# Two MoE layers behind attention, one core: conversions tied in place, stores and first loads divided

## The chip, the cores and the metric

One core of a Trainium2 chip runs the kernel. The metric is the device time of one execution in microseconds. Three executions of the kernel before took 878.22 us in the median (874.89 to 879.35).

## What is computed

Attention of four batches, eight heads and 32 global and 512 local tokens: each local token sees the global ones and a window of 32 to either side, each global token sees all. Its output, 2176 rows of 512, goes through two feed-forward layers (512 to 2048 to 512), all in float32. The weights arrive as float64 words, which the kernel turns into float32 itself.

```python
x = out_attention.transpose(0, 2, 1, 3).reshape(B * S, H * D)
h = x @ moe_w_in
x = (np.maximum(h, 0) + alpha * np.minimum(h, 0)) @ moe_w_out
h = x @ moe2_w_in
out = (h * np.clip(h + 3, 0, 6) / 6) @ moe2_w_out
```

## The kernel before

Products are made of values split into a high and a low part (`wt[:, m, 0]`, `wt[:, m, 1]`), three matmuls for each product. The 2176 tokens go through layer 1 in five blocks of 512, 512, 512, 256 and 384 columns (`blocks`, L331). The main loop (L779) runs, for each block, 16 chunks of the hidden size: `h_tile` (L365), `act` (L371 to L385) and, LAG = 2 steps later, `y_tiles` (L396). Block 0 has two lanes of 256 columns, the second DELAY = 4 steps behind the first (steps 4 to 15 run both), since its tokens' attention ends later. At step 4 the loop finishes that attention and transposes its output (L796 to L798).

Attention (`local_units`) works on 32 units of loads q, k and v, scores, exponentials, transposes, a copy of these to SBUF (L209) and values; `attention_steps` advances it between the chunks. All first loads are issued by SyncE's queue (SP), in the order of L231 to L239.

**Conversions.** A half chunk of weights is loaded as int64 words into one of four buffers `raw` (L97). `to_float32` then takes ScalarE L108 and VectorE L111, L112 and L114; L120 and L121 (layer 1) or L460 and L463 (layer 2) split the result `z` (two buffers). Layer 1's 32 halves are converted in block 0 by `Weights.convert`: of the two that belong to a step one is written ahead of `h_tile` and one behind `act`, two steps before they are used. Layer 2's conversions are a generator, `second_weights`, of 159 steps: 6 to begin with, then 13 for each of eight in-parts, then three (convert, high part, low part) for each of 16 `out_parts`, and a last one for the last store; each conversion stores its result to DRAM. `SPLIT` gives the steps of each block, spread evenly over the block's loop. A buffer `raw` is free again when L114 has read it (layer 1) or when its store has landed (layer 2). In block 4 `inputs` also reads the stored results of blocks 0 to 2 back into `xq` and splits them (L562, L563).

**Order.** Each engine runs its instructions in one order, and so does SP's queue of DMAs. That order is a planner's: it lists what is written, estimates times of its own, and issues next what it believes to be ready, earliest written first. `tc.keep_in_program_order(ins)` adds one edge: `ins` comes behind the instruction that was written just before it on its engine. In the kernel before, `second_weights` hands it to `to_float32` as `here`; `split_w` (layer 1) doesn't, so there L108 and L111 are free to go ahead.

**Stores.** At the end of a block, two L833 stores write four column groups of `x2` to DRAM. At the end of layer 2, `to_rows` copies each PSUM bank to SBUF (`evacuate`: ScalarE for even places, VectorE for odd ones) and stores it; the last three are the global rows "g" (four batches of 32 rows, L644), (3, 1, 0) and (3, 1, 1) (L648).

Of the kernel before, what the change touches and what calls it, by code (L numbers as in the profile page):

```python
# [10 lines left out]
F32R = mybir.dt.float32r  # L11
# [6 lines left out]
B, H, SL, SG, D = 4, 8, 512, 32, 64  # L18
# [6 lines left out]
W = 32  # L25
# [9 lines left out]
FIRST_UNITS = HP  # L35
# [4 lines left out]
DELAY = 4  # L40
STEPS = [[2] * 4 + [1] * 16, [1] * 16, [1] * 16, [2] * 16, [0] * 16]
CONVERT = (5, 7, 9)
SPLIT = (0, 46, 46, 30, 37)
STREAM = 4


# [6 lines left out]
def fused_kernel(ctx, tc, qT, kE, vE, qgT, kN, vN, vgN, w1, alpha, w2, mask, ident, out):  # L53
    nc = tc.nc
# [14 lines left out]
    spare = {"y": True, "n": 0}  # L69

    def load_constants():
        nc.sync.dma_start(out=mask_sb, in_=mask)
        nc.sync.dma_start(out=ident_sb, in_=ident)
        nc.sync.dma_start(out=alpha_sb, in_=alpha)
        nc.vector.tensor_scalar(out=c1_sb, in0=alpha_sb, scalar1=-1.0, scalar2=1.0, op0=ALU.mult, op1=ALU.add)

# [20 lines left out]
        nc.sync.dma_start(out=raw, in_=src[j, :, 512 * m:512 * m + 512])  # L97
        return raw

    def to_float32(raw, here=lambda ins: ins):  # L100

        words = raw.bitcast(U32).rearrange("p (f two) -> p f two", two=2)
        low, high = words[:, :, 0], words[:, :, 1]
        here(nc.scalar.activation(low, low, AF.Relu, bias=quarter_sb, scale=0.9 * 2.0 ** -29))  # L108
        z = work.tile([128, 512], F32, tag="z", name="z", bufs=ZB)
        bits = z.bitcast(U32)  # L110
        here(nc.vector.tensor_scalar(out=z, in0=high.bitcast(F32), scalar1=2.0 ** -112, scalar2=None, op0=ALU.mult))  # L111
        nc.vector.scalar_tensor_tensor(out=bits, in0=bits, scalar=3, in1=low, op0=ALU.logical_shift_left,  # L112
                                       op1=ALU.bitwise_or)
        nc.vector.scalar_tensor_tensor(out=bits, in0=high, scalar=0x80000000, in1=bits, op0=ALU.bitwise_and,  # L114
                                       op1=ALU.bitwise_or)
        return z
# [41 lines left out]
    def local_units(att):  # L158
        units = [(b, hf, hp) for b in range(B) for hf in range(2) for hp in range(HP)]
        q_t, k_t, v_t, p_t, rs_t, pt_t = {}, {}, {}, {}, {}, {}  # L160
        def load(u):
            b, hf, hp = units[u]
            q_t[u] = att.tile([128, 256], F32, tag="q", name="q_t", bufs=PRE + 1)
            nc.sync.dma_start(out=q_t[u], in_=qT[b, hp, :, 256 * hf:256 * hf + 256])
            k_t[u] = att.tile([128, UNIT_K], F32, tag="kE", name="k_t", bufs=PRE + 1)
            nc.sync.dma_start(out=k_t[u], in_=kE[b, hp, :, 384 * hf:384 * hf + UNIT_K])

# [280 lines left out]

    def second_weights():

        here = tc.keep_in_program_order
        todo = [(j, 0) for j in range(NJ)] + [(j, 1) for j in range(NJ)]
        raws, pending = [], []

# [21 lines left out]

        fetch()  # L480
        yield
        fetch()
# [1 line left out]
            yield  # L484
        for m in range(NP):
            own = raws.pop(0)
            z0, own = to_float32(own, here), own.bitcast(F32R)
            yield
            high(z0, own)
            yield  # L490
            low(z0, own, in_parts[m][:, 0])
            yield
            own = raws.pop(0)
            z1, own = to_float32(own, here), own.bitcast(F32R)
            store()
            yield
            high(z1, own)
            yield
            low(z1, own, in_parts[m][:, 1])
            yield  # L500
            a, b, c, d = z0[:, 0:256], z0[:, 256:512], z1[:, 0:256], z1[:, 256:512]
            add(d, c, d)
            add(c, a, c, ALU.subtract)
            store()
            yield
            st = parts_tile()
            high(z1, st)
            yield
            low(z1, st, in_parts[m][:, 2])
            fetch()  # L510
            yield
            add(a, d, a, ALU.subtract)
            add(b, b, a, ALU.subtract)
            store()
            yield
            st = parts_tile()
            high(z0, st)
            yield
            low(z0, st, in_parts[m][:, 3])
            fetch()  # L520
            yield
            store()
            yield
        for j in range(NJ):
            own = raws.pop(0)
            z, own = to_float32(own, here), own.bitcast(F32R)
            store()
            yield
            high(z, own)
            fetch()  # L530
            yield
            low(z, own, out_parts[j])
            yield
# [105 lines left out]
    def to_rows(y, tiles, order=None):  # L639
        for c in order or range(len(tiles)):  # L640
            tile_ = tiles[c]
            r = evacuate(y[c], c, 512, ("t", "z"))
            if tile_ == "g":
                nc.sync.dma_start(out=rows[:, 0:SG, :], in_=r)  # L644
            else:
                bb, hf, i = tile_
                at = SG + 256 * hf + 128 * i
                nc.sync.dma_start(out=rows[bb, at:at + 128, :], in_=r)  # L648
# [130 lines left out]
    for bi in range(len(blocks)):  # L779
# [49 lines left out]
        for c in range(0, NC, 2):  # L829
            r = work.tile([128, 2, 512], F32, tag="g", name="ev", bufs=LAG + 1)[:, :, :n]  # L830
            nc.scalar.copy(r[:, 0, :], y[c][:, :n])
            nc.vector.tensor_copy(r[:, 1, :], y[c + 1][:, :n])
            nc.sync.dma_start(out=x2[bi][:, c:c + 2, :], in_=r)  # L833
        xt = xt_next

    second_layer(bt)
# [56 lines left out]
```

## Time and profile before

| | us |
|---|---|
| median of three executions | 878.22 |
| lowest, highest | 874.89, 879.35 |
| the profiled execution | 876.12 |
| its span, first to last instruction | 874.3 |
| TensorE matmul busy | 843.5 (96%) |
| VectorE busy | 527.2 (60%) |
| ScalarE busy | 388.9 (44%) |

Engines: PE is TensorE's matmuls, PEld its weight loads, DVE is VectorE, ACT is ScalarE, SP is SyncE, SPq its queue of DMA issues. L108 is line 108 of the kernel. A row of waits gives who waited for whom. A DMA share of 1 would be all of the core's 16 DMA engines busy.

### The profile page before, as it was taken

How to read it: one execution, taken by the hardware profiler on the slowest of the kernel's cores; microseconds unless marked ns; L12 is line 12 of the kernel's file. 1: busy time of each engine (PE TensorE's matmuls, PEld its weight loads, DVE VectorE, ACT ScalarE, POOL GpSimd, SP SyncE). 2: the span in 40 equal slices, each digit the busy share in tenths (PEclk: the TensorE clock that was granted, in tenths of full speed). 3: DMA queues.
4: the chain of work that ended last, by engine and by line, in shares of the span. 5: the costliest groups of instructions: out<-in, count | busy, mean ns of one | idle time of the engine just before them, and what ended most of it. 6: DMA issues, size and time to landing. Idle time of an engine off the chain costs nothing.

```text
span 874.3 us, 17112 instructions
## 1 busy us (share of the span) xinstructions
PE 843.5 (96%) x6728; PEld 731.1 (84%) x6728; DVE 527.2 (60%) x1267; ACT 388.9 (44%) x893; POOL 0.2 (0%) x4
## 2 busy tenths in 40 slices
PE   7889989999999999999999999999999999999996
PEld 5679989877887878788999977888888999988995
DVE  5989885565567556576687975766720766701321
ACT  6767564454445444354555543433410444401221
POOL 0000000000000000000000000000000000000000
PEclk8889999999999999999999999999999999999998
DMA  9986662335547451688766577666786888788781
GB/s 315 322 277 211 203 221 86 132 98 197 180 150 264 163 169 74 233 306 280 266 227 213 183 250 266 220 208 219 239 300 219 275 269 299 266 307 296 251 255 41
DMA packets 63875, 195.63 MB, mean 224 GB/s; under 512 B 7220, under 2 KB 19764, under 8 KB 62772
## 3 DMA queue, kind: packets, MB, share of 16 engines
q1 hardware_dynamic: 63796, 194.55, 66.5%
q8 instruction: 53, 0.87, 0.4%
q14 instruction: 26, 0.21, 0.1%
HBM read 160.44 MB, written 34.08 MB: 222 GB/s over the span
## 4 chain that ended last, share of the span: by engine, by line
PE 75%; DMA 11%; DVE 8%; ACT 4%; issue 1%; SPq 1%; ACTq 0%; DVEq 0%
PE o_ps L636 21%; PE h_ps L365 15%; PE y_ps L396 14%; PE k_ps L690 14%; DMA raw<-in_w 5%; PE h_ps L755 4%; DMA wo<-raw 3%; PE s_ps L184 2%; DVE z L112 1%; PE o_ps L219 1%; PE pt_ps L207 1%; DVE z L114 1%; DVE t L377 1%; ACT raw L108 1%; DMA ws<-wi 1%
## 5 line engine op out<-in xcount | busy, mean ns | idle before, releaser
L396 PE MATMUL y_ps<-g,wt 128*128 128x256 f32 (+2 forms) x1152 | 212.4, 334 | 7.2 <-ACT g L383 7.2
L365 PE MATMUL h_ps<-xt,wt 128*128 128x256 f32 (+2 forms) x1152 | 209.9, 333 | 3.7 <-DVE t L377 3.0
L365 PEld LDWEIGHTS h_ps<-xt,wt 128*128 128x128 f32 x1152 | 181.3, 194 | 20.6 <-ACT wt L120 3.2
L396 PEld LDWEIGHTS y_ps<-g,wt 128*128 128x128 f32 x1152 | 175.3, 190 | 26.8 <-ACT g L383 8.9
L690 PE MATMUL k_ps<-bt,ws 128*128 128x512 f32 (+1 forms) x672 | 140.6, 363 | 0.0
L690 PEld LDWEIGHTS k_ps<-bt,ws 128*128 128x128 f32 x672 | 121.9, 188 | 15.0 <-issue 0.4
L636 PE MATMUL o_ps<-ws,g 128*128 128x512 f32 x480 | 117.8, 391 | 1.6 <-DMA ws<-wo 1.6
L636 PEld LDWEIGHTS o_ps<-ws,g 128*128 128x128 f32 x480 | 89.6, 188 | 19.3 <-DMA ws<-wo 2.1
L377 DVE SCALAR_TENSOR_TENSOR t<-t,c_sb,h_ps 128x256 f32<-128x256 f32 (+2 forms) x96 | 55.4, 589 | 76.9 <-ACT t L375 76.9
L375 ACT ACTIVATE t<-h_ps 128x512 f32<-128x512 f32 (+2 forms) x84 | 43.1, 515 | 83.2 <-PE h_ps L365 83.1
L636 PE MATMUL o_ps<-ws,far 128*128 128x512 f32 x336 | 76.8, 389 | 0.0
L636 PEld LDWEIGHTS o_ps<-ws,far 128*128 128x128 f32 x336 | 63.1, 188 | 13.1
L383 ACT CAST g<-t 128x512 fp32r<-128x512 f32 (+2 forms) x84 | 45.2, 538 | 41.9 <-DVE t L377 39.9
L108 ACT ACTIVATE raw<-raw,quarter_sb 128x512 uint32<-128x512 uint32 x64 | 49.0, 768 | 28.4 <-DMA raw<-in_w 28.4
L384 DVE TENSOR_TENSOR g<-t,g 128x512 fp32r<-128x512 f32 (+2 forms) x84 | 49.2, 586 | 19.2 <-ACT g L383 19.1
L628 ACT ACTIVATE t<-cd,half_sb 128x512 f32<-128x512 f32 (+1 forms) x32 | 21.5, 671 | 72.6 <-DVE cd L675 71.6
L196 ACT ACTIVATE p<-p,st 128x128 f32<-128x128 f32 x128 | 49.9, 391 | 7.1 <-DVE st L192 7.0
L112 DVE SCALAR_TENSOR_TENSOR z<-z,raw 128x512 uint32<-128x512 uint32 x64 | 44.0, 688 | 2.2 <-ACT raw L108 0.9
L405 DVE COPY ev<-o_ps 128x512 f32<-128x512 f32 x7 | 4.8, 690 | 66.7 <-PE o_ps L636 66.7
L114 DVE SCALAR_TENSOR_TENSOR z<-raw,z 128x512 uint32<-128x512 uint32 x64 | 43.9, 686 | 0.6
L630 ACT CAST g<-t 128x384 fp32r<-128x384 f32 (+1 forms) x48 | 26.3, 549 | 26.4 <-DVE t L629 26.4
L631 DVE TENSOR_TENSOR g<-t,g 128x384 fp32r<-128x384 f32 (+1 forms) x48 | 28.8, 600 | 12.4 <-ACT g L630 11.3
(97 smaller groups left out, 822.8 us busy)
## 6 DMA issues: line engine op xcount, KB each, us to landing
ws<-wi SPq DMA_DIRECT2D x80, 512.0 KB, 5.0
ws<-wo SPq DMA_DIRECT2D x80, 512.0 KB, 4.6
raw<-in_w SPq DMA_DIRECT2D x64, 512.0 KB, 4.7
v_t<-in_vE SPq DMA_DIRECT2D x32, 512.0 KB, 5.1
wi<-raw SPq DMA_DIRECT2D x16, 512.0 KB, 3.0
wi<-parts SPq DMA_DIRECT2D x16, 512.0 KB, 4.1
wo<-raw SPq DMA_DIRECT2D x16, 512.0 KB, 5.0
k_t<-in_kE SPq DMA_DIRECT2D x32, 240.0 KB, 4.1
```

The source lines that it names most:

```text
L108: here(nc.scalar.activation(low, low, AF.Relu, bias=quarter_sb, scale=0.9 * 2.0 ** -29))
L112: nc.vector.scalar_tensor_tensor(out=bits, in0=bits, scalar=3, in1=low, op0=ALU.logical_shift_left, op1=ALU.bitwise_or)
L114: nc.vector.scalar_tensor_tensor(out=bits, in0=high, scalar=0x80000000, in1=bits, op0=ALU.bitwise_and, op1=ALU.bitwise_or)
L196: nc.scalar.activation(p[:, n, :], p[:, n, :], AF.Exp, bias=st[:, 1, n:n + 1], scale=-1.0, accum_out=st[:, 2, n:n + 1])
L365: nc.tensor.matmul(ps[:, a:b], lhsT=wts[j][:, 0, wl, 128 * c:128 * c + 128], rhs=xt[c][:, xl, a:b], start=k == 0, stop=k == 3 * NC - 1)
L375: nc.scalar.activation(t[:, a:b], ps[:, a:b], AF.Relu, scale=-1.0)
L377: nc.vector.scalar_tensor_tensor(out=t[:, c:d], in0=t[:, c:d], scalar=c1_sb[:, j:j + 1], in1=ps[:, c:d], op0=ALU.mult, op1=ALU.add)
L383: nc.scalar.copy(g[:, 0, a:b], t[:, a:b])
L384: nc.vector.tensor_tensor(out=g[:, 1, a:b], in0=t[:, a:b], in1=g[:, 0, a:b].bitcast(F32), op=ALU.subtract)
L396: nc.tensor.matmul(y[c][:, a:b], lhsT=wts[j][:, 1, wl, 128 * c:128 * c + 128], rhs=g[:, gl, a:b], start=first, stop=last)
L636: nc.tensor.matmul(y[c], lhsT=g[:, gl, 128 * c:128 * c + 128], rhs=wo[:, wl, :], start=j == 0 and (wl, gl) == (0, 0), stop=j == NJ - 1 and ...
L690: nc.tensor.matmul(bank, lhsT=wt[:, wl, at:at + 128], rhs=bt[x][:, c, xl, 0:w], start=k == 0, stop=k == 5)
```

## The change

`here` becomes the tie for every call of `to_float32`, layer 1's too. `SPLIT` moves twelve steps of `second_weights` from block 4 to blocks 1 and 2. `mask`, `ident` and the q loads of the first four units are issued by ScalarE's queue in place of SP's. The store of the global rows becomes four stores of 32 rows, on SP and ScalarE in turn, and each store of two `x2` column groups becomes two.

```diff
-SPLIT = (0, 46, 46, 30, 37)
+SPLIT = (0, 52, 52, 30, 25)
...
     def load_constants():
-        nc.sync.dma_start(out=mask_sb, in_=mask)
-        nc.sync.dma_start(out=ident_sb, in_=ident)
+        nc.scalar.dma_start(out=mask_sb, in_=mask)
+        nc.scalar.dma_start(out=ident_sb, in_=ident)
         nc.sync.dma_start(out=alpha_sb, in_=alpha)
...
-    def to_float32(raw, here=lambda ins: ins):
+    here = tc.keep_in_program_order
+
+    def to_float32(raw):
...
         def load(u):
             b, hf, hp = units[u]
             q_t[u] = att.tile([128, 256], F32, tag="q", name="q_t", bufs=PRE + 1)
-            nc.sync.dma_start(out=q_t[u], in_=qT[b, hp, :, 256 * hf:256 * hf + 256])
+            early = nc.scalar if u < FIRST_UNITS else nc.sync
+            early.dma_start(out=q_t[u], in_=qT[b, hp, :, 256 * hf:256 * hf + 256])
...
-            z0, own = to_float32(own, here), own.bitcast(F32R)
+            z0, own = to_float32(own), own.bitcast(F32R)
...
             if tile_ == "g":
-                nc.sync.dma_start(out=rows[:, 0:SG, :], in_=r)
+                for b in range(B):
+                    queue = nc.scalar if b % 2 else nc.sync
+                    queue.dma_start(out=rows[b, 0:SG, :], in_=r[W * b:W * b + W, :])
...
-            nc.sync.dma_start(out=x2[bi][:, c:c + 2, :], in_=r)
+            for i in range(2):
+                nc.sync.dma_start(out=x2[bi][:, c + i, :], in_=r[:, i, :])
```

## Rows read from the trace of the kernel before

**Rows 1.** The page, busy tenths in 40 slices of the span: TensorE.

```profile
PE   7889989999999999999999999999999999999996
```

**Rows 2.** Stages: from:to length, busy PE PEld DVE ACT POOL, clock, DMA share, GB/s.

```profile
24.00:57.00 33.00, 29.39 (x443) 23.55 (x443) 30.59 (x106) 24.12 (x72) 0.00 (x0) 0.91 0.89 305
57.00:136.00 79.00, 73.89 (x854) 70.95 (x854) 68.44 (x176) 51.25 (x121) 0.00 (x0) 0.96 0.63 205
136.00:160.00 24.00, 24.00 (x363) 22.79 (x362) 10.28 (x46) 10.95 (x38) 0.00 (x0) 1.00 0.34 109
160.00:372.00 212.00, 212.00 (x1891) 170.43 (x1889) 124.41 (x332) 100.10 (x249) 0.00 (x0) 1.00 0.50 168
430.00:530.00 100.00, 94.06 (x516) 88.67 (x515) 82.59 (x151) 51.89 (x99) 0.00 (x0) 0.98 0.71 237
```

**Rows 3.** Waits, 0:136 us, then 430:530: total, times, longest.

```profile
ACT raw L108 <- DMA raw<-in_w: 22.7, 19, 2.8
...
ACT bt L562 <- DMA xq<-x: 8.5, 2, 4.7
ACT raw L108 <- DMA raw<-in_w: 5.7, 2, 5.0
```

**Rows 4.** Timeline, TensorE: start, length, work, [idle before <- what ended it].

```profile
7.77 0.64 PE L184 MATMUL s_ps<-k_t,q_t 64*32 64x128 f32 x16 [2.04 <-DMA k_t<-in_kE]
34.23 1.21 PE L396 MATMUL y_ps<-g,wt 128*128 128x256 f32 x8 [1.04 <-ACT g L383]
58.35 1.54 PE L350 MATMUL xt_ps<-ident_sb,xo 128*128 128x128 f32 x6 [3.05 <-ACT pt L209]
...
126.85 1.43 PE L365 MATMUL h_ps<-xt,wt 128*128 128x256 f32 x10 [3.00 <-DVE t L377]
```

**Rows 5.** Timeline, ScalarE, in front of three of these.

```profile
31.86 0.76 ACT L108 ACTIVATE raw<-raw,quarter_sb 128x512 uint32<-128x512 uint32 x1 [0.77 <-DMA raw<-in_w]
...
57.08 0.74 ACT L108 ACTIVATE raw<-raw,quarter_sb 128x512 uint32<-128x512 uint32 x1 [2.77 <-DMA raw<-in_w]
...
124.57 0.74 ACT L108 ACTIVATE raw<-raw,quarter_sb 128x512 uint32<-128x512 uint32 x1 [2.21 <-DMA raw<-in_w]
```

**Rows 6.** Groups: count | busy, mean ns; L120: min/median/max ns, first, last start.

```profile
L112 DVE SCALAR_TENSOR_TENSOR z<-z,raw 128x512 uint32<-128x512 uint32 x64 | 44.0, 688 | 2.2 <-ACT raw L108 0.9
...
L111 DVE TENSOR_SCALAR z<-raw 128x512 f32<-128x512 f32 x64 | 26.8, 419 | 0.0
...
L120 ACT CAST wt<-z x32: 600/608/633, 16.1 to 134.3; 128x512 fp32r<-128x512 f32 x32
```

**Rows 7.** Timeline, TensorE, block 4.

```profile
482.52 3.06 PE L396 MATMUL y_ps<-g,wt 128*128 128x384 f32 x12 [1.91 <-ACT g L383]
...
508.68 2.37 PE L396 MATMUL y_ps<-g,wt 128*128 128x384 f32 x12 [1.88 <-ACT g L383]
...
527.98 2.34 PE L636 MATMUL o_ps<-ws,g 128*128 128x512 f32 x9 [1.64 <-DMA ws<-wo]
```

**Rows 8.** Timeline, first loads, ScalarE's first exponential; a window as in rows 2.

```profile
1.64 0.43 SPq L72 DMA_DIRECT2D mask_sb<-in_mask  x1
...
3.53 0.43 SPq L166 DMA_DIRECT2D k_t<-in_kE  x1
...
6.34 0.40 ACT L196 ACTIVATE p<-p,st 128x128 f32<-128x128 f32 x1 [4.34 <-DVE st L192]
...
4.00:6.00 2.00, 1.73 (x34) 0.65 (x32) 0.13 (x1) 0.00 (x0) 0.00 (x0) 1.00 0.88 202
```

**Rows 9.** Tail: last issues; windows as in rows 2; L648's landing near 674.

```profile
867.38 0.94 SPq L648 DMA_DIRECT2D out<-ev  x2
...
870.00:871.00 1.00, 0.00 (x0) 0.00 (x0) 0.00 (x0) 0.00 (x0) 0.00 (x0) 0.50 0.88 301
871.00:872.00 1.00, 0.00 (x0) 0.00 (x0) 0.00 (x0) 0.00 (x0) 0.00 (x0) 0.50 0.29 104
...
DMA to landing us min/median/max: 2.9/3.0/3.0
```

More of the change, by code (lines that the diff above doesn't have):

```diff
@@ L449, in second_weights @@
     def second_weights():
-        here = tc.keep_in_program_order
         todo = [(j, 0) for j in range(NJ)] + [(j, 1) for j in range(NJ)]
@@ L493, in second_weights @@
             own = raws.pop(0)
-            z1, own = to_float32(own, here), own.bitcast(F32R)
+            z1, own = to_float32(own), own.bitcast(F32R)
             store()
@@ L525, in second_weights @@
             own = raws.pop(0)
-            z, own = to_float32(own, here), own.bitcast(F32R)
+            z, own = to_float32(own), own.bitcast(F32R)
             store()
```

## The prediction

> **What bounds the kernel now.** I read the page's slices first: TensorE is at 9 tenths in almost every slice [rows 1]. So time can only be won where TensorE stands still or runs on the lower clock. The table by stage says where that is [rows 2]: 160 to 372 us is full, as is what lies behind 530 us [rows 1]; 24 to 57 us lose 3.6 us, 57 to 136 us lose 5.1 us and have a mean clock of 0.96, 430 to 530 us lose 5.9 us and have 0.98. Before 24 us and behind the last matmul lie the start and the tail.
>
> The waits of the two poor stages name the suspect [rows 3]: up to 136 us ScalarE waited 22.7 us in 19 pieces for raw weights (L108, the first step of a conversion), more than for anything else there; from 430 to 530 us it waited 5.7 us for raw weights and 8.5 us for the blocks that `inputs` reads back (L562). TensorE's own idle rows show when that hurts [rows 4]: 1.04 us before 34.23, 3.05 us before 58.35, 3.00 us before 126.85. Each has, on ScalarE just ahead, an L108 that waited for a raw landing: 0.77, 2.77 and 2.21 us [rows 5]. Counting L108 and L209 in the order of the code, the L108 at 57.08 is the fourteenth, written behind step 5's activation, and the copy L209 that it held up is written in step 4. At 57 us four L108 had run ahead of their place. That is the planner at work: L108 and L111 depend on a load alone, so it puts them wherever it believes the load has landed.
>
> **The change part by part.** Sums go against the profiled execution: 876.12 us, of which 874.3 is the span; it lies 2.1 us under the median of the three (878.22), so the same sum is taken from the median.
>
> *Ties of layer 1's conversions.* No instruction is added. L108 and L111 of the 32 conversions may no longer run ahead of the instruction written before them on ScalarE and VectorE. Where a free L108 waits for its load, the activations, attention copies and exponentials of its step stand queued behind it, and TensorE waits for those; a tied one stands behind them, and what waits for it is h two steps on. The raw load that takes over its buffer is issued later too, and on SP's queue q, k and v of units two ahead stand behind that load: 0 (+1). Early: the 1.04 us before 34.23 goes, since the L108 in front (0.77 of waiting and 0.76 of work, [rows 5]) is then written behind step 1's activation: -1.0 us (0 to -1.0). The 3.05 us before 58.35: the conversion is written a step behind the copy, so the copy isn't held: -3.0 us (0 to -3.05). The rest of 57 to 136 us: 3.7 us of TensorE idle behind 58.35 and 0.04 x 79 = 3.2 us of clock, 6.9 us to be had. VectorE sets a floor there. A conversion costs it 0.42 + 3 x 0.69 = 2.48 us (L111, L112 and two more like L112) [rows 6]. It was busy for 68.4 of the 79 us [rows 2]. Two conversions that ran ahead (`z` has two buffers, so their VectorE part can't run further ahead) now fall into this stage: 68.4 + 5.0 = 73.4 us. Unless work slips behind 136 us, where VectorE was busy for only 10.3 of 24 us [rows 2], the stage can't be shorter than that: at most -5.6 us, of which 1.4 are already counted before 58.35, so -4.2 to 0. I take two thirds, -2.8: it reached 93% at most over such a stretch (30.6 of 33 us, [rows 2]), so the floor itself won't be met without that slip. New waits from the new order of everything: the nearest rows are the present idle times of 1 to 3 us [rows 4]; one of the size in between, +2.0 us (0 to +6).
>
> *Split of layer 2's conversion.* Twelve of the 159 steps leave block 4 (37 to 25), six each go to blocks 1 and 2. Block 2 then ends at step 104 of the 110 that make the in-parts, and block 4 keeps eight `out_parts` conversions where it had twelve. That takes 4 x 2.48 = 9.9 us of VectorE and 4 x (0.76 + 0.61) = 5.5 us of ScalarE [rows 5, 6] out of 430 to 530 us (VectorE 82.6 of 100 us [rows 2]) and four raw loads and four stores out of SP's queue. In blocks 1 and 2 VectorE was busy for 124.4 of 212 us with TensorE never idle, so it costs 0 there (cover gone: +2). In block 4 three idle times of TensorE hang on the same traffic [rows 7]: 1.91 us (ScalarE stood behind `xq`, whose load stood in SP's queue behind a raw load that waits for a store's landing), 1.88 us (ScalarE stood 5.0 us behind a raw load [rows 3]) and 1.64 us (the first `ws`, in a raw buffer whose last store had not landed). With one conversion every 2.2 steps of the loop instead of 1.5, a store has half as long again to land before its buffer is asked for. With the rest of the 5.9 us and 0.02 x 100 = 2 us of clock, 7.9 us hang there. The last conversion still falls in the last step of the loop, so the third wait shrinks rather than goes: -4.0 us (0 to -7.9).
>
> *First loads from two engines.* q of units 0 to 3, mask and ident are issued by ScalarE, which stood idle for 4.34 us before its first exponential at 6.34 [rows 8]; six issues at SP's 0.43 us are hidden. On SP the second k moves from seventh place (3.53 us) to third (1.64 us) [rows 8]; TensorE waited 2.04 us for it [rows 4]. Next late are the bytes: the DMA engines were 0.88 busy already between 4 and 6 us [rows 8], so what waits for a v or a raw later lands little sooner. So -0.8 us (+0.5 to -2.0).
>
> *Smaller stores.* The two `x2` stores of a block become four: ten more SP issues of 0.33 to 0.47 us, while SP mostly waits: 0 (+1). The tail matters: the last two stores are issued from 867.38 to 868.32 us [rows 9], the second from about 867.85, and the span ends at 874.3. From 870 to 871 us the DMA engines were 0.88 busy, from 871 to 872 only 0.29 [rows 9]: about a quarter of them works on, as if the "g" store (one store whose output starts with a dimension of 4) lay on 4 of 16 engines and the other two stores had their shares behind it. Around 674 us a store of L648 lands 2.9 to 3.0 us after its issue [rows 9]; here the span's end comes 6.4 us after it. Four stores of 32 rows each can lie on all 16: the last lands at 867.85 + about 0.1 (one issue more on SP) + 3.0 + up to 0.8 for sharing, and the span ends as far behind that as now, some 1 us: 872.0 to 872.8 where it was 874.3: -1.9 us (-2.4 to -0.7, the latter if ScalarE's two issues, 0.4 us each, delay the copy of the second tile). A rule speaks against it: the Trainium skill ("DMA: Bandwidth & Descriptors", section "Bandwidth") gives a 64 KB transfer 0.95 us at 32% efficiency and asks for 1 MiB. An estimate by that page: four would take 3.8 us one after another, and the tail would gain nothing.
>
> Sum: -1.0 - 3.0 - 2.8 + 2.0 - 4.0 - 0.8 - 1.9 = -11.5 us. 876.1 - 11.5 = 864.6 for an execution like the profiled one, 878.2 - 11.5 = 866.7 for the median.
>
> **The rivals.**
> 1. VectorE takes over in block 0 (17%): conversions then follow at VectorE's pace. In this trace 32 conversions took 16.1 to 134.3 us, 3.8 us each [rows 6], 7.6 us for the two that belong to each step of the loop. Nothing is won up to 136 us apart from the start, and half in block 4: -1.9 - 0.8 - 2.0 = -4.7, 873.5 us. For it: 68.4 of 79 us busy. Against: part of those 3.8 us was ScalarE's waiting (22.7 us, [rows 3]), which goes.
> 2. The ties don't do it (10%): they hold two of five instructions and no load. Layer 2's L108 is tied already, and two of them still waited 5.7 us [rows 3]. Then only start, tail and block 4 are won: -6.7, 871.5 us.
> 3. Everything comes (8%): all the far ends, -1.0 - 3.05 - 4.2 - 7.9 - 2.0 - 2.4 = -20.6 us and no new wait, 857.7 us.
> 4. Slower (7%): the lead was needed. A tied conversion starts behind step s's activation and its weights are wanted at step s + 2. If L108 and L112 (0.76 + 0.69 us) lie bare in each of the twelve two-lane steps (4 to 15), TensorE waits 12 x 1.45 = 17.4 us at h for `wt`; less 6.7 for the other parts, 889 us. It decides from the point where a conversion behind step s's activation takes longer than that step's and the next one's matmuls; its own chain is 0.76 + 3 x 0.69 + 0.61 = 3.4 us, about half of a step (7.6 us for two conversions above), so VectorE's queue has to add a whole step to it.
> 5. The small stores don't shorten the tail (8%): four issues, four completions, and the bytes end as late as now; then 866.7 + 1.9 = 868.6 us, with 0.45 us for the issues 869. The Trainium skill's page cited above ("DMA: Bandwidth & Descriptors", section "Bandwidth") speaks for it; no row here shows a store of 64 KB. Against: the idle DMA engines at 871 us.
>
> **How the numbers follow.** 50% for the sum, 866.7 us. Between rival 3 and rival 1 with its spread lie about eight tenths: 858 to 876. A difference of 0.5% (4.4 us) is about what can be told here. Faster than 873.8: the forecast but for its edge, rivals 2, 3 and 5 and half of rival 1: 0.80. Slower than 882.6: rival 4, 0.07. Same: 0.13.
>
> **What would show it.** Right: no L108 with a landing as its releaser up to 136 us in front of L209 or L375; ScalarE's 22.7 us under 5; no idle time over 1 us in TensorE's rows from 30 to 136; VectorE over 90% there; `xq` and raw waits of block 4 under 5 us together; the last store landing within 4 us of its issue; the second k's scores right behind the first. Wrong: TensorE idle at L365 with `wt` L121 or L120 as the releaser (rival 4); L108 waits as before in other places (rival 2); new idle times between 160 and 430 us, where there is none to win; a DMA share of a quarter at the end (rival 5).

## The result and the profile after

| | before | after |
|---|---|---|
| median of four executions each, us | 878.79 | 868.93 |
| lowest to highest | 874.89 to 879.85 | 867.82 to 869.74 |
| profiled execution; its span | 876.12; 874.3 | 869.12; 867.3 |
| last matmul's end to the span's end | 8.0 | 5.0 |

The changed kernel takes 0.9895 of the time, with an interval of 0.9862 to 0.9928: 9.9 us by the medians, 7.0 us by the two profiled executions. The sum had been 11.5 us.

Stages of the changed kernel, with the columns of [rows 2] and in its order; the row from 372 us is new:

```profile
24.00:57.00 33.00, 29.91 (x474) 23.47 (x475) 29.53 (x106) 24.71 (x79) 0.00 (x0) 0.95 0.79 257
57.00:136.00 79.00, 75.32 (x886) 69.72 (x886) 70.18 (x179) 52.67 (x119) 0.00 (x0) 1.00 0.65 216
136.00:160.00 24.00, 24.00 (x335) 22.93 (x335) 13.79 (x53) 11.96 (x40) 0.00 (x0) 1.00 0.36 115
160.00:372.00 212.00, 212.00 (x1891) 170.52 (x1889) 130.73 (x344) 103.30 (x255) 0.00 (x0) 1.00 0.53 182
372.00:430.00 58.00, 55.68 (x765) 48.07 (x764) 38.63 (x118) 29.74 (x78) 0.00 (x0) 1.00 0.82 277
430.00:530.00 100.00, 98.49 (x559) 93.91 (x559) 77.72 (x139) 48.31 (x95) 0.00 (x0) 1.00 0.65 223
```

The last row is the one that changed most: TensorE busy for 98.5 of 100 us where it was 94.1, VectorE for 77.7 where it was 82.6. Windows of equal time don't hold equal work, though. To see where time went, take the moment at which TensorE has done the same amount of work in both profiled executions, and subtract (plus: the changed kernel is later):

| stretch of the kernel before | forecast | by the traces |
|---|---|---|
| start to 25 us | -0.8 | +1.1 |
| 25 to 60 us (the waits of 1.04 and 3.05) | -4.0 | -2.4 |
| 60 to 140 us (with the new waits) | -0.8 | +1.7 |
| 140 to 360 us | 0 | 0.0 |
| 360 to 430 us (block 3) | 0 | +2.4 |
| 430 to 530 us (block 4) | -4.0 | -7.3 |
| 530 to 866 us | 0 | +0.5 |
| tail | -1.9 | -3.0 |
| sum | -11.5 | -7.0 |

So the total was nearer than its parts. In block 0 one trace is a rough measure. The kernel before, traced a second time (below), is 2.9 us behind its own first trace at 55 us and 0.7 at 140 us; behind block 0 the two stay within 0.7 us of each other. And five kernels below (without the new split, with more of it, with the global rows in one store or in two, with the x2 stores in pairs) run block 0 in the changed kernel's order on TensorE, VectorE and ScalarE, yet are 0.8 to 2.8 us behind the kernel before at 140 us, where the changed kernel is 0.4. From 60 to 140 us they lose 1.7 to 4.1 us, so its +1.7 is the low end.

Part of the spread is TensorE's clock. In four of the five it is on the lower of its two levels (1.2 and 2.4 GHz) for 3.4 us, from 0.6 to 1.5 us behind the wait of 1.92 us shown below; in the changed kernel's trace and in the one with more of the split it stays at 1.00 there. With the x2 stores in pairs (the last three figures: granted clock, DMA share, GB/s) it is 0.72 over six microseconds, by estimate up to 1.7 us of work (0.28 x 6):

```profile
72.00:78.00 6.00, 5.79 (x35) 5.65 (x36) 4.46 (x8) 1.83 (x4) 0.00 (x0) 0.72 0.52 161
```

Waits of ScalarE in the kernel before, 0 to 136 us (one row that [rows 3] doesn't have), then in the changed kernel, 0 to 136 us and 430 to 530 us (total, times, longest), and TensorE's idle rows of block 0:

```profile
ACT wt L120 <- DVE z L114: 5.9, 6, 1.5
...
ACT wt L124 <- DVE z L118: 9.7, 10, 1.8
...
ACT raw L112 <- DMA raw<-in_w: 8.1, 6, 2.7
...
ACT bt L566 <- DMA xq<-x: 5.9, 2, 3.2
...
34.55 0.64 PE L190 MATMUL s_ps<-k_t,q_t 64*32 64x128 f32 x16 [1.26 <-ACT pt L215]
...
59.50 2.66 PE L371 MATMUL h_ps<-xt,wt 128*128 128x256 f32 x20 [0.89 <-DVE xt L343]
...
72.24 0.39 PE L371 MATMUL h_ps<-xt,wt 128*128 128x256 f32 x1 [1.92 <-ACT wt L124]
```

ScalarE's waits for raw weights went from 22.7 us in 19 pieces [rows 3] to 8.1 in 6, and the 3.05 us before 58.35 and 3.00 before 126.85 [rows 4] are gone. In their place h now waits for `wt`: 1.92 us in one piece, behind it a row of waits of 0.1 to 0.2 us at L371 and L402, 2.8 us in all from 57 to 136 us. That is rival 4's sign at a sixth of its 17.4 us. The rows on L124 (L120 before) say why: ScalarE's last step of a conversion waits for VectorE's last step of it, 9.7 us in all where it was 5.9. The 1.26 us before 34.55 is of the same kind, since L215 stood there behind an L124 that had waited 1.84 us for VectorE; with 0.61 us before 35.80 it stands in the place of the 1.04 us before 34.23. ScalarE's first step of the conversion that the 1.92 us hang on, then VectorE in front of that wait:

```profile
63.17 0.77 ACT L112 ACTIVATE raw<-raw,quarter_sb 128x512 uint32<-128x512 uint32 x1
...
68.00 0.42 DVE L115 TENSOR_SCALAR z<-raw 128x512 f32<-128x512 f32 x1
68.34 0.29 DVE L198 CUSTOM_DVE_ANT_0 p<-s_ps,mask_sb 128x128 f32<-128x128 f32 x1
...
69.18 0.42 DVE L229 TENSOR_TENSOR xo<-o_ps,rs 128x256 f32<-128x256 f32 x1
69.52 0.69 DVE L390 TENSOR_TENSOR g<-t,g 128x512 fp32r<-128x512 f32 x1
70.12 0.69 DVE L116 SCALAR_TENSOR_TENSOR z<-z,raw 128x512 uint32<-128x512 uint32 x1
...
70.84 0.69 DVE L118 SCALAR_TENSOR_TENSOR z<-raw,z 128x512 uint32<-128x512 uint32 x1
```

It is the twelfth conversion. ScalarE's L112 for it ends at 63.94, but VectorE's first step, L115, starts at 68.00, behind step 4's activation (L383, L390), where its tie puts it: 4.1 us. It ends at 68.42; then four masks of the attention (L198), its output (L229) and an activation's low part (L390) run, and the second step starts at 70.12: 1.7 us more. From L112 to the end of L124 the conversion takes 9.0 us; the prediction had 3.4 us for its own work. Each of the two delays is about the size of the wait or larger, and how much of either would have to go isn't shown.

In block 4, TensorE has one idle time over 1 us left, where it had three of 1.6 to 1.9 [rows 7]:

```profile
451.53 1.68 PE L402 MATMUL y_ps<-g,wt 128*128 128x384 f32 x8 [1.21 <-ACT g L389]
```

ScalarE stood 3.6 us there until an `x2` store let a buffer go. The tail: the last issues, and the DMA engines (share of 16, then GB/s) while they end:

```profile
862.59 0.81 SPq L651 DMA_DIRECT2D out<-ev  x2
863.49 0.88 SPq L655 DMA_DIRECT2D out<-ev  x2
...
865.00:866.00 1.00, 0.00 (x0) 0.00 (x0) 0.00 (x0) 0.00 (x0) 0.00 (x0) 0.99 0.91 346
866.00:867.00 1.00, 0.00 (x0) 0.00 (x0) 0.00 (x0) 0.00 (x0) 0.00 (x0) 0.50 0.01 4
```

From 0.91 the share falls to 0.01 at once, without the step at 0.29 of [rows 9]. The last store lands 2.5 us after its issue (863.96 to 866.48), where it took 5.4.

### The profile page after: what moved, and what is told of

Its sections match the earlier page's. It is cut to its first block, busy times and chain, and to the rows that moved or that the text cites. A ratio compares the mean times of both kernels' runs of the same rounds, so it can differ in the third digit from the quotient of the medians.

```text
span 867.3 us, 17114 instructions
## 1 busy us (share of the span) xinstructions
PE 847.6 (98%) x6728; PEld 729.8 (84%) x6728; DVE 529.8 (61%) x1267; ACT 388.8 (45%) x893; POOL 0.2 (0%) x4
## 4 chain that ended last, share of the span: by engine, by line
PE 82%; DVE 8%; DMA 5%; ACT 3%; issue 1%; ACTq 0%; SPq 0%
PE o_ps L640 21%; PE y_ps L402 18%; PE h_ps L371 17%; PE k_ps L697 15%; PE h_ps L762 4%; DMA raw<-in_w 2%; PE s_ps L190 2%; DVE z L116 1%; PE pt_ps L213 1%; PE o_ps L225 1%; DVE z L118 1%; DVE wt L125 1%; DVE z L115 1%; DMA x<-ev 1%; ACT wt L124 1%
## 5 line engine op out<-in xcount | busy, mean ns | idle before, releaser
L402 PE MATMUL y_ps<-g,wt 128*128 128x256 f32 (+2 forms) x1152 | 213.0, 334 | 3.5 <-ACT g L389 2.6
L371 PE MATMUL h_ps<-xt,wt 128*128 128x256 f32 (+2 forms) x1152 | 209.9, 331 | 2.8 <-ACT wt L124 1.9
L402 PEld LDWEIGHTS y_ps<-g,wt 128*128 128x128 f32 x1152 | 175.5, 189 | 24.1 <-ACT g L389 3.5
L371 PEld LDWEIGHTS h_ps<-xt,wt 128*128 128x128 f32 x1152 | 178.7, 191 | 19.6 <-ACT wt L124 2.3
L383 DVE SCALAR_TENSOR_TENSOR t<-t,c_sb,h_ps 128x256 f32<-128x256 f32 (+2 forms) x96 | 55.5, 589 | 66.5 <-ACT t L381 66.3
L390 DVE TENSOR_TENSOR g<-t,g 128x512 fp32r<-128x512 f32 (+2 forms) x84 | 49.1, 585 | 22.0 <-ACT g L389 21.1
L112 ACT ACTIVATE raw<-raw,quarter_sb 128x512 uint32<-128x512 uint32 x64 | 49.6, 775 | 8.4 <-DMA raw<-in_w 8.3
L202 ACT ACTIVATE p<-p,st 128x128 f32<-128x128 f32 x128 | 50.0, 394 | 6.7 <-DVE st L198 6.5
```

Source lines behind the costliest of these rows:

```text
L202: nc.scalar.activation(p[:, n, :], p[:, n, :], AF.Exp, bias=st[:, 1, n:n + 1], scale=-1.0, accum_out=st[:, 2, n:n + 1])
L371: nc.tensor.matmul(ps[:, a:b], lhsT=wts[j][:, 0, wl, 128 * c:128 * c + 128], rhs=xt[c][:, xl, a:b], start=k == 0, stop=k == 3 * NC - 1)
L383: nc.vector.scalar_tensor_tensor(out=t[:, c:d], in0=t[:, c:d], scalar=c1_sb[:, j:j + 1], in1=ps[:, c:d], op0=ALU.mult, op1=ALU.add)
L390: nc.vector.tensor_tensor(out=g[:, 1, a:b], in0=t[:, a:b], in1=g[:, 0, a:b].bitcast(F32), op=ALU.subtract)
L402: nc.tensor.matmul(y[c][:, a:b], lhsT=wts[j][:, 1, wl, 128 * c:128 * c + 128], rhs=g[:, gl, a:b], start=first, stop=last)
```

## Experiments

### One part taken out at a time

Four kernels, each the changed kernel with one part undone; 879.82 us was the median of the kernel before beside them (18 executions, 875.0 to 883.8). What a part is worth is the difference to the changed kernel's median of 868.93 us. By the ratios to the kernel before the three that cost time come out lower (4.0 us for the ties, 3.0 for the split, 2.2 for the small stores), and their intervals overlap the changed kernel's; but none of their executions is as fast as its slowest (869.74).

**Without the ties of layer 1**

```diff
-    def to_float32(raw):
+    def to_float32(raw, here=lambda ins: ins):
...
-            z0, own = to_float32(own), own.bitcast(F32R)
+            z0, own = to_float32(own, here), own.bitcast(F32R)
```

> The changed kernel with layer 1's conversions free again, all else as changed. The changed kernel's own executions: 868.9 us. Theory A (the ties won the waits before 60 us and lost most of it again between 60 and 140 us, where weights now come just in time): idle times of about 3 us return near 55 and 124 us, ScalarE's wait for raw weights up to 136 us rises from 8 to over 18 us, the waits of 0.2 to 2 us for wt go; in sum 869 to 871 us. Theory B (the ties are worth what was forecast for them, 6.8 us): 875 to 876 us.

873.88 us (871.1 to 878.6), 0.994 of the kernel before (0.9913 to 0.9967): the ties are worth 5.0 us in the changed kernel, between the two theories. Its trace shows the forecast's mechanism coming back. ScalarE, then TensorE, near 60 us; ScalarE's wait for raw weights up to 136 us is 26.3 us in 18 pieces:

```profile
60.09 0.77 ACT L112 ACTIVATE raw<-raw,quarter_sb 128x512 uint32<-128x512 uint32 x1 [2.86 <-DMA raw<-in_w]
60.76 0.57 ACT L215 COPY pt<-pt_ps 128x512 f32<-128x512 f32 x1
...
61.38 1.97 PE L356 MATMUL xt_ps<-ident_sb,xo 128*128 128x128 f32 x8 [2.67 <-ACT pt L215]
```

L112 stands 2.86 us behind a load with the copy L215 queued behind it, and TensorE waits 2.67 us for that copy. By 140 us this kernel is 6.1 us behind the kernel before, which has no such ties either; what differs in block 0 are the first loads alone. The planner's order of block 0 is another there on TensorE, VectorE and ScalarE. So without ties an edit to the start reorders all of block 0, here at a cost of some 6 us in this one trace; the kernels here with ties and the old lead end block 0 0.4 to 2.8 us behind.

**Without the new split**

```diff
-SPLIT = (0, 52, 52, 30, 25)
+SPLIT = (0, 46, 46, 30, 37)
```

> The changed kernel with SPLIT as before (37 steps in block 4). Theory A (the split won the whole of block 4's idle time, 7.3 us from 430 to 530, and cost 2.4 us in block 3): block 4 has 5 to 6 us of idle time again, block 3 loses less, 868.9 + 7.3 - 2.4 = 873.8 us. Theory B (the split won the forecast 4.0 us, block 3's loss has another cause): 872.9 us with block 3 as in the changed kernel. Theory C (the idle times of block 4 went through the new order of stores and not the split): 868 to 870 us.

872.78 us (870.7 to 876.1), 0.9929 (0.991 to 0.9947): the split is worth 3.9 us. TensorE in block 4, and ScalarE's waits there:

```profile
508.31 3.74 PE L402 MATMUL y_ps<-g,wt 128*128 128x384 f32 x12 [1.86 <-ACT g L389]
...
ACT bt L566 <- DMA xq<-x: 7.9, 2, 3.9
ACT raw L112 <- DMA raw<-in_w: 4.2, 2, 3.5
```

The waits of [rows 7] and [rows 3] are back in the main: TensorE's three are 1.13, 1.86 and 0.53 us where they were 1.91, 1.88 and 1.64. And block 3 ends as in the kernel before (0.0 us where the changed kernel loses 2.4). So the split both wins in block 4 (7.3 us with it, 1.2 us without) and costs in block 3.

**Without the first loads from ScalarE**

```diff
-        nc.scalar.dma_start(out=mask_sb, in_=mask)
-        nc.scalar.dma_start(out=ident_sb, in_=ident)
+        nc.sync.dma_start(out=mask_sb, in_=mask)
+        nc.sync.dma_start(out=ident_sb, in_=ident)
...
-            early = nc.scalar if u < FIRST_UNITS else nc.sync
+            early = nc.sync
```

> The changed kernel with q, mask and ident on SP's queue again. Theory A (two queues made the start slower, since q of unit 1 now travels beside the first v and lands at 8.2 us in place of 6.3): unit 1's scores start before 8.0 us, TensorE is 1 us further at 25 us, 867 to 868 us. Theory B (the forecast: two queues are worth 0.8 us): 869 to 870 us, and the second k is waited for again, until 7.6 us.

868.80 us (867.6 to 871.2), 0.9888 (0.986 to 0.9916): worth nothing. Its trace is 0.8 to 1.3 us ahead of the changed kernel's from 25 to 30 us and level with it (+0.4 both) at 140 us. Between them lie more waits for `wt` (4.2 us from 57 to 136, the changed kernel 2.8) and 3.4 us on the lower clock right behind the longest of them, which the changed kernel's trace doesn't have.

**Without the four small stores**

```diff
-                for b in range(B):
-                    queue = nc.scalar if b % 2 else nc.sync
-                    queue.dma_start(out=rows[b, 0:SG, :], in_=r[W * b:W * b + W, :])
+                nc.sync.dma_start(out=rows[:, 0:SG, :], in_=r)
```

> The changed kernel with the global rows stored in one piece again. Theory A (that store keeps a quarter of the DMA engines busy alone and the two others behind it): from TensorE's end to the span's end 8.0 us in place of 5.0, 871.9 us. Theory B (the tail is short for another reason, as two queues of stores or the order of copies): 5 to 6 us, 869 us.

871.44 us (870.7 to 874.2), 0.992 (0.9892 to 0.9949): 2.5 us by the medians, and a tail of 7.9 us in the trace against 5.0: theory A.

### Ties alone, x2 stores alone, the store's shape

**The ties alone**, on the kernel before.

```diff
+    here = tc.keep_in_program_order
+
-    def to_float32(raw, here=lambda ins: ins):
+    def to_float32(raw):
...
```

> The kernel before with nothing but the ties of layer 1's conversions (split, loads and stores as before). Theory A (the prediction's terms: -1.0, -3.0, -2.8, +2.0): 4.8 us faster than the kernel before in the same runs, 874 to 876 us where that has about 879 to 880. Theory B (the ties pay back what they win: in the changed kernel's trace block 0 ends 0.4 us later than in the kernel before, and without the first loads from ScalarE likewise): within 1 us of the kernel before, 878.5 to 880.5 us, and in the trace TensorE's 3.05 us ahead of 58 us gone, with new waits for wt of as much behind it.

875.58 us (873.1 to 879.7) beside 878.15 (14 executions): 0.9972 (0.9951 to 0.9994), so 2.6 us, between the two theories. TensorE's idle rows behind 57 us:

```profile
59.12 2.65 PE L367 MATMUL h_ps<-xt,wt 128*128 128x256 f32 x20 [0.26 <-DVE xt L339]
71.84 0.39 PE L367 MATMUL h_ps<-xt,wt 128*128 128x256 f32 x1 [1.91 <-ACT wt L122]
94.23 0.39 PE L367 MATMUL h_ps<-xt,wt 128*128 128x256 f32 x1 [0.45 <-ACT wt L122]
133.96 0.74 PE L398 MATMUL y_ps<-g,wt 128*128 128x256 f32 x4 [0.65 <-ACT wt L122]
```

By the traces it gains 4.1 us between 55 and 60 us and is 1.2 us behind by 140 us: the waits for `wt` come with the ties, not with the loads or the split.

**The x2 stores in pairs again**

```diff
-            for i in range(2):
-                nc.sync.dma_start(out=x2[bi][:, c + i, :], in_=r[:, i, :])
+            nc.sync.dma_start(out=x2[bi][:, c:c + 2, :], in_=r)
```

> The changed kernel with the stores of x2 in pairs of column groups again. Theory A (they are worth nothing, as forecast): every stage's end within 0.5 us of the changed kernel's, the span 866.5 to 868.5 us. Theory B (the single stores let inputs start sooner in block 4, a part of the gain there): block 4 ends 1 to 3 us later, ScalarE waits longer for xq, span 868.5 to 870.5. Theory C (the ten issues more stand in front of raw loads): 0.5 to 1.5 us faster.

869.11 us in one execution, the span 867.3 us as with the change, and no stage's end off by more than 1.6 us (theory A had said 0.5): worth nothing, as forecast.

**The global rows in two stores of two batches**

```diff
-                for b in range(B):
-                    queue = nc.scalar if b % 2 else nc.sync
-                    queue.dma_start(out=rows[b, 0:SG, :], in_=r[W * b:W * b + W, :])
+                for b in range(0, B, 2):
+                    nc.sync.dma_start(out=rows[b:b + 2, 0:SG, :], in_=r[W * b:W * b + 2 * W, :])
```

> The changed kernel with the store of the global rows as two stores of two batches (64 rows, 128 KB each), both on SP, in place of four of one batch on two queues. From the last matmul's end to the span's end it was 8.0 us with one store of four batches and 5.0 us with four stores. Theory A (a store lies on as many DMA engines as its outer dimension allows: four with one store of four batches, two with a store of two batches, all 16 with one batch): the two stores lie on two engines each, and the tail is at least as long as with one store, 8 to 11 us. Theory B (smaller stores end sooner by their size): between the two, 5.5 to 7 us. Theory C (what helped was the second queue): about 6 to 8 us with both stores spread over all engines.

875.53 us in one execution, the tail 10.8 us: longer than with one store. The DMA engines in this tail (the last two figures: share of 16, GB/s):

```profile
866.00:867.00 1.00, 0.00 (x0) 0.00 (x0) 0.00 (x0) 0.00 (x0) 0.00 (x0) 0.50 0.75 268
867.00:868.00 1.00, 0.00 (x0) 0.00 (x0) 0.00 (x0) 0.00 (x0) 0.00 (x0) 0.50 0.53 166
868.00:869.00 1.00, 0.00 (x0) 0.00 (x0) 0.00 (x0) 0.00 (x0) 0.00 (x0) 0.50 0.32 121
869.00:870.00 1.00, 0.00 (x0) 0.00 (x0) 0.00 (x0) 0.00 (x0) 0.00 (x0) 0.50 0.15 49
870.00:871.00 1.00, 0.00 (x0) 0.00 (x0) 0.00 (x0) 0.00 (x0) 0.00 (x0) 0.50 0.12 43
871.00:872.00 1.00, 0.00 (x0) 0.00 (x0) 0.00 (x0) 0.00 (x0) 0.00 (x0) 0.50 0.14 53
```

Twice the stores at half the size end later: for three microseconds 0.12 to 0.15 of 16 engines work, about two, so both stores lie on the same two. One store of four batches left 0.29, about four [rows 9]; four stores of one batch ended on all of them. Theory A stands: what counts is the store's outer dimension, and a smaller store is not faster by its size. The Trainium skill ("DMA: Bandwidth & Descriptors", section "Why a DMA increments its semaphore by 16 and not by 1") says of the outer dimension that a DMA lies on the largest number of engines up to 16 that divides the slowest dimension of both sides. The shares above agree with it. Whether four stores of one batch on SP alone end as early as on two queues was not tried.

### Can the waits for wt be had back?

**A lead of three steps from the start**

```diff
-AHEAD = 2
+AHEAD = 3
```

> The changed kernel with AHEAD = 3: layer 1's tied conversions are written three steps ahead of their use in place of two. In the changed kernel's trace TensorE waits for the split weights wt between 68 and 134 us, about 2.8 us of idle time (1.92 us in one piece) and 5.4 us with the spacing around it. Theory A (the tie takes the lead away, rival 4's mechanism at a smaller price): the waits for wt go, block 0 ends 2 to 4 us earlier, median 865 to 867 us. Theory B (block 0 goes at VectorE's or ScalarE's pace, rival 1): the waits move to activations, g or the attention's exponentials, block 0 ends within 1 us of before, 868 to 870. Theory C (the first steps get one conversion more ahead of the attention): new idle time ahead of 60 us, 870 to 873.

872.89 us (872.3 to 874.3), 0.9955 of the kernel before (0.9933 to 0.9978), so about 5 us lost against the changed kernel's 0.9895 (4.0 by the medians): theory C, with a half of A true. From 57 to 136 us nothing waits for `wt` any more, and the stretch from 60 to 140 us comes out 3.8 us shorter than in the changed kernel. But ScalarE earlier:

```profile
50.64 0.78 ACT L112 ACTIVATE raw<-raw,quarter_sb 128x512 uint32<-128x512 uint32 x1 [4.06 <-DMA raw<-in_w]
51.88 0.76 ACT L112 ACTIVATE raw<-raw,quarter_sb 128x512 uint32<-128x512 uint32 x1 [0.46 <-DMA raw<-in_w]
52.55 0.38 ACT L202 ACTIVATE p<-p,st 128x128 f32<-128x128 f32 x1
```

A tied L112 asks for weights that haven't landed, and the exponentials L202 stand behind it: the old stall, now written into the program order. At 55 us it is 10.9 us behind the kernel before (the changed kernel 2.9).

**A lead that grows from step 4 on**

```diff
-                    W1.convert(min(1, W1.needed(s + AHEAD) - W1.next))
+                    lead = min(W1.needed(s + AHEAD) + min(2, max(0, s - DELAY + 1)), 2 * NJ)
+                    W1.convert(min(1, lead - W1.next))
...
-                    W1.convert(W1.needed(s + AHEAD) - W1.next)
+                    W1.convert(lead - W1.next)
```

> The changed kernel with a lead of layer 1's tied conversions that grows once block 0's second lane has begun: two steps ahead up to step 3, half a step more at step 4, a whole step more (three steps) from step 5 on. With three steps from the start, TensorE's waits for wt behind 62 us were gone (that stretch to 140 us came out 3.8 us shorter than in the changed kernel), but ahead of 55 us ScalarE stood 4.06 us behind a raw load with exponentials queued behind it, and 8 to 10 us were lost there. Theory A (the lead is too short only once the attention's start is over): up to 58 us as in the changed kernel, behind it no wait for wt over 0.5 us, block 0 ends 2 to 4 us earlier, median 865 to 867 us. Theory B (block 0 goes at the pace of loads or VectorE, whatever the lead): the waits move to other places, 868 to 870 us.

872.82 us (868.5 to 874.8), 0.9925 of the kernel before (0.9902 to 0.9949), not better either. TensorE's waits, 57 to 136 us:

```profile
PE h_ps L371 <- ACT wt L124: 4.6, 3, 1.7
```

4.6 us in three pieces (changed kernel: 1.9 in one). The waits moved, as theory B says, but the time lies outside both theories. VectorE is busy for 69 of 79 us there, and the two extra conversions fall into these steps. That they push the others back, so that a lead must be won before it can be spent, is an argument and not shown: with three steps from the start VectorE was busy for 71 of the same 79 us, and TensorE waited for no `wt`.

**More of the split**

```diff
-SPLIT = (0, 52, 52, 30, 25)
+SPLIT = (0, 60, 60, 20, 19)
```

> The changed kernel with SPLIT = (0, 60, 60, 20, 19): eight more steps of layer 2's conversion each in blocks 1 and 2, ten fewer in block 3, six fewer in block 4. Theory A (what counts is how many conversions, three steps each among the out_parts and 6.5 each among the in-parts, fall into the stages where TensorE waits; blocks 1 and 2 hide them): block 3, in which the changed kernel fell 2.4 us behind, wins 1 to 2.5 us, block 4 wins 0 to 1.5, 160 to 372 us stay full, median 865 to 867.5 us. Theory B (block 3's loss is the global rows' attention alone, block 4 has nothing left): within 1 us, 868 to 870. Theory C (blocks 1 and 2 fill up): new idle time of TensorE between 160 and 372 us, 870 or more.

869.47 us (868.6 to 871.7), 0.9901 (0.9869 to 0.9932), the same as the changed kernel: theory B. Block 4 keeps six of layer 2's conversions (the changed kernel eight, the kernel before twelve) and 160 to 372 us stay full, VectorE at 138 of 212 us; block 4 wins 1.3 us more, and 140 to 360 us lose 0.8. Block 3 still loses 2.1 us, in another way: TensorE stands idle there for 1.69 us ahead of one group of the score matmuls shown below.

### Block 3

The 2.4 us lost there show in the score matmuls of the global rows. TensorE, changed kernel, then without the new split:

```profile
384.48 1.09 PE L287 MATMUL gs_ps<-gk,gq 64*32 64x512 f32 x16
397.48 1.06 PE L287 MATMUL gs_ps<-gk,gq 64*32 64x512 f32 x8
398.79 1.06 PE L287 MATMUL gs_ps<-gk,gq 64*32 64x512 f32 x8
411.65 1.06 PE L287 MATMUL gs_ps<-gk,gq 64*32 64x512 f32 x8
413.20 1.06 PE L287 MATMUL gs_ps<-gk,gq 64*32 64x512 f32 x8
...
397.34 1.09 PE L287 MATMUL gs_ps<-gk,gq 64*32 64x512 f32 x16
410.54 1.09 PE L287 MATMUL gs_ps<-gk,gq 64*32 64x512 f32 x16
```

Sixteen passes (records of the trace) in one piece take 1.09 us, eight take 1.06. In the changed kernel the planner put matmuls of y into the middle of two such groups, and each half costs as much as a whole: by equal work 1.0 us is lost at each of the two, the other 0.5 us between 374 and 380 us. In all eight kernels here with the changed kernel's split two groups are torn, in all five with the old one none. With still more of the split none is torn either and block 3 loses nearly as much, so tearing is one form of the loss and not the only one. I took the two heads' turn-about order for the reason and tried that by itself.

**The heads one after the other**, on the kernel before.

```diff
-            for b in range(B):
-                for h in range(2):
+            for h in range(2):
+                for b in range(B):
                     nc.tensor.matmul(s[h][W * b:W * b + W, :], lhsT=q[64 * h:64 * h + 64, W * b:W * b + W],
```

> The kernel before with the eight score matmuls of the global rows (64 rows of the array for each of two heads, four batches each) written one head after the other in place of turn and turn about. In the kernel before all 16 passes of them end in 1.09 us, four times over; in the changed kernel two of these four groups are torn into two of 8 passes of 1.06 us each with y's matmuls between them, and block 3 falls 2.4 us behind. Theory A (the two heads lie on two halves of the array's rows and run at the same time only when they are issued next to each other): each group of 16 takes 2.0 to 2.2 us, block 3 ends 3 to 5 us later, span 877 to 879.5. Theory B (what costs is the change between these small matmuls and y's, so that two groups cost two changes): a group of 16 in one piece still takes 1.1 to 1.3 us, block 3 within 1 us.

```profile
397.67 1.09 PE L281 MATMUL gs_ps<-gk,gq 64*32 64x512 f32 x16
410.67 1.09 PE L281 MATMUL gs_ps<-gk,gq 64*32 64x512 f32 x16
```

Theory A fell: the group still takes 1.09 us, and block 3 ends where it did (0.4 us less far behind than at its begin; one execution, 879.41 us beside 882.08). The order inside the group doesn't matter, only that it is in one piece. The Trainium skill ("TensorE: Matmul & The Clock Gate", section "Part 3: Packing small matmuls — row/col tiling") says that matmuls at different places of the array run at the same time; the trace agrees, with 16 passes as cheap as 8. Why another split of the conversions makes the planner tear the groups isn't shown.

### The kernel before, once more

No edit.

> The kernel before once more, with a profile, since its first profiled execution (876.12 us) lies 2 to 4 us below its medians (878.2 to 879.8 us), while the changed kernel's profiled execution lies at its median. Theory A (executions of the kernel before differ in block 0, where nothing ties its conversions): 877 to 881 us, later than the first one by 1 to 5 us by the end of block 0, in other waits for raw or stretches of lower clock. Theory B (they differ elsewhere, or the first trace is typical): block 0's end within 0.5 us of the first one's.

875.84 us: nearest to theory B. At 140 us it is 0.7 us behind its first trace (theory B had said 0.5), at the end 0.3 us ahead, in the same order of instructions in block 0. So both traces of the kernel before lie near 876 us, while 45 executions of it beside the experiments took 874.4 to 883.8, with medians of 878.2, 879.1 and 879.8. What it does in the longer ones no trace here shows. The granted clock doesn't tell either: 0.980 to 0.993 over the whole span in the 45, 0.984 and 0.985 in the traced ones. Those 2.9 us of the gain (9.9 by the medians, 7.0 by the traces) stay open.

## Why the prediction was right, and where it wasn't

The forecast of 866.7 us is 2.2 us off, and 868.93 lies well inside 858 to 876. That it came so near is partly luck. Between like executions, the profiled ones, it was 864.6 against 869.12: the start, the ties, block 3 and what lies behind 530 us fell short of their terms by 8.9 us together, block 4 and the tail beat theirs by 4.4. And 2.9 us of the gain by the medians show in no trace. Point by point:

- *Ties, -4.8 together.* The first half of the mechanism was right: with the ties ScalarE no longer stands behind loads with L215 behind it (8.1 us of waits for loads in place of 22.7), and without them the same stall is back (2.86 and 2.67 us at 60 us). The size by the medians: 5.0 us in the changed kernel, 2.6 us alone. But no trace of block 0 shows a gain over the kernel before: the kernels with ties and the old lead end it 0.4 to 2.8 us later, the two traces of the kernel before lie 0.7 us apart. Where the medians' gain falls stays open. The step that failed is the rest of 57 to 136 us, -2.8 and +2.0, which came out as +1.7 in this trace and up to +4.1 in others with the same order. The sum let VectorE fill its gaps; in the trace the tie holds the conversion's first step on VectorE back by 4.1 us, other work in its queue the second by 1.7, and h waits for `wt`. That was rival 4, priced at 17.4 us for a bare 1.45 us in each of twelve steps; it cost 2.8 us of idle time. Its point of decision, VectorE's queue adding a step to the chain, is what the rows at 63 to 72 us show. Idle time alone doesn't make the +1.7, since the kernel before stood idle for 3.7 us there; the rest lies in matmuls that follow each other more slowly: the weight loads of y waited 2.6 us for `wt` in nine pieces, where the kernel before shows none. Nor did the 1.04 us before 34.23 go (-1.0 forecast).
- *Split, -4.0.* 3.9 us by the medians. By the traces it is -7.3 in block 4 where the kernel with the old split has -1.2, and +2.4 in block 3: 6.1 won and 2.4 lost, the right sum of two terms of which one was too small and the other missing. The forecast counted twelve steps out of block 4 and held block 3 for untouched because its number stayed 30. The planner's order there changed nonetheless, in all eight kernels with the new split and in none of the five with the old.
- *First loads, -0.8.* Nothing measured (868.80 without). The second k moved ahead as forecast (landing 5.5 us, before 7.6), but the second q came last: TensorE waits 2.63 us for q where it waited 2.04 us for k [rows 4]. The prediction looked at k alone: it said of v and raw that the bytes come late whatever the order, and q was not counted among them. Behind that wait TensorE has a granted clock of 0.51 from 9 to 23 us, nearly all of it on the lower level, where it had 0.76 before and has 0.74 without this part; at 20 us it is 4.3 us behind the kernel before, at 25 us 1.1, since the kernel before waits 1.97 us for a v at 24.15.
- *Tail, -1.9.* 3.0 us by the traces, 2.5 by the medians. The mechanism, four engines under one store, is shown by the shares of 0.29, 0.12 to 0.15 and 0.01; the size was off because a last store landed 2.5 us after its issue and not 3.0 and 0.8 for sharing. Rival 5 is out: four stores of 64 KB landed within 1.7 to 2.0 us of their issue, overlapping. By the prediction's estimate from the Trainium skill ("DMA: Bandwidth & Descriptors", section "Bandwidth") four would take 3.8 us one after another; the four here had all landed 2.4 us after the first was issued.
- *x2 stores, blocks 1 and 2, 0.* As forecast: 212.0 of 212 us with VectorE at 130.7.

Of the seven signs that were to show it, five missed: waits for raw 8.1 us for under 5, idle times of 1.26 and 1.92 us in block 0 for none over 1, VectorE 89% for over 90, `xq` 5.9 us for under 5, and the second k's scores 2.63 us behind the first, waiting for q. All but `xq`'s told of a gain that was smaller, at its place, than the term in the sum; block 4 won more than its term in spite of that sign. Of the signs against it rival 4's came, TensorE idle at h for `wt`.

No kernel tried here beats the changed one by more than can be told; without the first loads, with more of the split and (one execution) with the x2 stores in pairs the time is the same.

## What to carry to other kernels

Tying a step to its place stops it from blocking the queue early, and makes it late instead: look, before counting the gain, which engine's queue stands between its first and its last instruction. Where a planner orders the work, an edit in one stage can cost or win in another that it doesn't touch, so a part's value is measured by taking it out of the finished kernel as well as by adding it to the old one; for the ties the two were 5.0 and 2.6 us. Give the last stores of a kernel an outer dimension that spreads over all DMA engines before anything else in its tail.

## What the hardware showed that I had not expected

- Small matmuls of 64 rows and 32 columns cost the same in eights and sixteens (1.06 and 1.09 us) if nothing stands between them; a group torn in two by other matmuls cost 1.0 us more, twice.
- Two stores in place of one can be slower: the tail was 8.0 us with one store of four batches, 10.8 with two of two, 5.0 with four of one.
- At the start it looks as if no more than eight DMAs can be under way, both queues together. SP's issues, ScalarE's, and TensorE's first wait for a load:

```profile
2.11 0.43 SPq L177 DMA_DIRECT2D v_t<-in_vE  x1
4.16 0.33 SPq L172 DMA_DIRECT2D k_t<-in_kE  x1
...
2.14 2.80 ACTq L170 DMA_DIRECT2D q_t<-in_qT  x3
...
8.36 0.64 PE L190 MATMUL s_ps<-k_t,q_t 64*32 64x128 f32 x16 [2.63 <-DMA q_t<-in_qT]
```

  Each queue issues four and stops. The ninth DMA, a q, is issued at 3.98 us, when the first k has landed (3.96), the tenth at 4.16 (a landing at 4.14), and so on. With all first loads on SP's queue (the kernel without this part) no more than eight are under way either. Whether the limit is the chip's or the program's isn't shown. The second q, 128 KB issued at 2.14 us on ScalarE's queue beside a v of 512 KB issued at 2.11 on SP's, landed at 8.22, behind that v (8.04): this small load on a queue of its own did not pass the large one.
